# Attention and two feed-forward blocks on one core: one Mish session for chunks 0 and 1, in-products of chunk 2 by quarters, first transfers from two queues, other places for the attention calls

## The chip, the cores and the metric

The kernel runs on one core of a Trainium2 chip. A core has four compute engines that this text needs: TensorE (PE, matrix products, with weight loads on PEld), VectorE (DVE), ScalarE (ACT) and GpSimd (POOL), and a queue engine, SyncE (SP), that issues transfers. Each runs its own instructions in order, and they wait for each other by semaphores. The metric is the device time of one execution in microseconds.

## The reference, cut to what is computed

```
scores = q @ k.T / 8                     # 4 batches, 8 heads, 576 x 576, head size 64
mask:  heads 0..3 local (the last 32 positions), heads 4..7 strided (same position mod 32, not later)
attn = softmax(masked scores) @ v        # -> x, 2304 tokens x 512
h = x @ w_in;  g = h * tanh(softplus(h)) # Mish, 2048 wide
x = g @ w_out                            # 512
out = (silu(x @ w_gate) * (x @ w_val)) @ w_out2    # 1536 wide
```

Weights and activations are 32-bit; products are made from a high and a low part of each operand, so one product of the algebra is three on TensorE (`mm3`: high by high, high by low, low by high).

## The kernel before

Attention goes in 24 steps of six or eight blocks of 64 queries (local steps have 96 keys in a block, strided steps 64). Batch b has steps 6b to 6b+5: three for heads 0 to 3 (local), three for heads 4 to 7 (strided), and in the last batch the strided ones come first. One call of `at_pair` is a software pipeline over steps: call k computes scores of step k (`at_qk`), maxima with the mask added (`at_max`, VectorE), exponentials (`at_exp`, ScalarE); normalises step k-1 (`at_add` on GpSimd, `at_norm`: a reciprocal on VectorE, two multiplications on GpSimd); transposes step k-2 (`at_tr`, `at_copy`); and multiplies step k-3 with v (`at_pv`), splitting the result into `xh` (`at_hi`, a cast on ScalarE) and `xl` (`at_lo`, a subtraction on VectorE). The list `PAIR` fixes the order of these in a call, and so the order on each engine. Scores have two banks (`sc`), so the scores of a call wait until the maxima of the call before are read.

The first feed-forward block works on five chunks of tokens (512 each, the last 256) and four quarters of the hidden width. n = 5q + c counts quarter and chunk. For n = 0, 1, 2 the work is woven into the attention calls: `g1_step(n, f, kc)` adds a quarter kc of the contraction to h of hidden tile f (three products), and after kc = 3 `act_a` takes h out of its bank, because Mish needs another table on ScalarE than exp. Three banks (`mm`) serve both h and the out-products y. h goes to a tile `u` (four buffers); `act_m` loads the Mish table, applies Mish to four tiles and loads exp again; `g_hi` and `g_lo` split the result; `g2_mm` multiplies it with the out-weight.

Calls 0 to 14 come in a loop in which the tables `WSTEPS` and `GROUPS` say how many weight operations (`w_step`: four per weight tile, on VectorE, and one square on ScalarE) and which g1 steps follow a call. `KEEP` and `NWARM` are counts of idle products (`spin`) that keep TensorE at work while it has nothing. `DOS` runs deferred steps from the list `todo` (Mish of chunk 0 among them) at places in calls 13 and 14. After that, `fill` runs ahead of each g1 step or after each g2 product, counts itself, starts a call where its count is in `PAIR_AT`, and runs one to three deferred steps. From n = 3 (chunk 3) on there is no attention left and products follow each other.

K and Q of a pair of heads lie in one of four buffers, which are those of the accumulators `acc0` to `acc3` (`load_qk`, L298); `acc0` holds its last K and Q in call 7. The first transfers are all issued by SyncE, the masks (`cst`) first (L818 to L829).

Names in rows: `sc` scores, `pt` and `sm` exponentials and sums, `tp` and `ts` transposes, `xp` the product with v, `w`, `wtmp` and `raw` a weight tile, its work buffer and its bits, `h`, `u`, `g`, `y` as above, `wp` the spins. L92 is `mm3`; L83 and L88 are the high and low split, of whichever tile.

Of the kernel before, what the change touches and what calls it, by code (L numbers as in the profile page):

```python
# [20 lines left out]
LK = LB + STR  # L21
# [17 lines left out]
NWARM = 10  # L39
KEEP = {0: 2, 1: 3, 2: 4, 3: 4}  # L40
QK_SLOT = (0, 1, 2, 3, 0, 1, 2, 3, 1, 2, 3, 1, 2, 3, 1, 2)
GROUPS = {
# [11 lines left out]
}  # L54
WSTEPS = (0, 0, 4, 4, 3, 3, 2, 0, 1, 1, 2, 2, 2, 2, 0)
WFILL = 6
DOS = {13: (0, 2), 14: (1, 0, 2, 2)}
PAIR_AT = (0, 5, 13, 16, 19, 22, 26, 30, 34, 38, 42, 47)
# [5 lines left out]
def local_strided_attention__mish_moe__swiglu_kernel(  # L64
# [241 lines left out]
    def load_v(s):  # L306
        b, first, g, part = steps[s]
        t = sb.tile([128, 2, 4, 128], F32, tag="v", name="v", bufs=2)
        n = len(part) // 2
        for x in range(2):  # L310
            v_t[s, x] = t[:128 if first else LK, x, :n]
            nc.sync.dma_start(v_t[s, x], (v_str if first else v_loc)[b, 2 * g + x, :, :n])
# [159 lines left out]
    def of(do, h):  # L472
# [6 lines left out]
        (at_add, -1),  # L479
        (at_pv, -3),  # L480
# [6 lines left out]
        (at_norm, -1),  # L487
# [7 lines left out]
    SPLIT = 8  # L495
# [20 lines left out]
    us, gt = {}, {}  # L516
# [19 lines left out]
    def act_a(n, f, keep):  # L536

        nt = CHUNKS[n % NCH][1]
        p = h_ps.pop((n, f))[:, :nt]
        us[n, f] = u = sb.tile([128, 512], F32, tag="u", name="u", bufs=4)[:, :nt]  # L540
        if keep:
            if n:
                nc.vector.tensor_copy(u, p)
            else:
                nc.scalar.copy(u, p)
        else:
            nc.scalar.activation(out=u, in_=p, func=AF.Mish)  # L547
# [257 lines left out]
    with tc.manual_schedule():  # L805
# [27 lines left out]
        def act_all(n):  # L833
            todo.append(lambda n=n: act_m(n))
            for f in range(QF):
                todo.append(lambda n=n, f=f: g_hi(n, f))
                todo.append(lambda n=n, f=f: g_lo(n, f))

        def g1_step(n, f, kc):
# [3 lines left out]
            if kc == 3:  # L843
                act_a(n, f, True)
                if n == 0 and f == QF - 1:
                    act_all(0)

        for k in range(len(WSTEPS)):
# [3 lines left out]
            dos = list(DOS.get(k, ()))  # L852
            for x in (None,) + GROUPS.get(k, ()):
                if x:
                    g1_step(*x)
                do(dos.pop(0) if dos else 0)
        fills = [0]

        def fill():
# [3 lines left out]
            if fills[0] < WFILL + 2:  # L863
                w_lo(nc.vector)
                w_hi()
                w_step(fills[0] < WFILL)
            fills[0] += 1
            do(3 if len(todo) > 10 else 2 if len(todo) > DO2 else 1)

        g1s = [(n, f, kc) for n, fs_ in ((1, (3,)), (2, range(QF))) for f in fs_ for kc in range(4)]  # L870
        g1s.insert(0, (1, 2, 3))
        wfill = [0]
        for n in range(1, 3):
# [3 lines left out]
            todo.append(lambda n=n: act_m(n))  # L877
# [188 lines left out]
```

## Time and profile before

| | |
|---|---|
| median of 3 runs | 900.97 us (900.77 to 901.16) |
| the profiled execution | 902.88 us |
| its span, first to last instruction | 901.1 us |
| TensorE busy | 879.2 us (98%) |
| VectorE, ScalarE, GpSimd busy | 585.3, 385.6, 137.2 us |
| mean granted clock of TensorE | 0.99 of full speed |

A row of the order of time gives the start and the duration in microseconds, the engine, the line, the operation, what it writes and reads, how many in a row, and in brackets how long the engine had been idle and what ended that. Busy time of a pipelined TensorE overlaps a little between groups, so starts are the safer numbers. Full speed is 2.4 GHz; the lower level is 1.2 GHz, and a mean between is a mix of both.

### The profile page before, as it was taken

How to read it: one execution, taken by the hardware profiler on the slowest of the kernel's cores; microseconds unless marked ns; L12 is line 12 of the kernel's file. 1: busy time of each engine (PE TensorE's matmuls, PEld its weight loads, DVE VectorE, ACT ScalarE, POOL GpSimd, SP SyncE). 2: the span in 40 equal slices, each digit the busy share in tenths (PEclk: the TensorE clock that was granted, in tenths of full speed). 3: DMA queues.
4: the chain of work that ended last, by engine and by line, in shares of the span. 5: the costliest groups of instructions: out<-in, count | busy, mean ns of one | idle time of the engine just before them, and what ended most of it. 6: DMA issues, size and time to landing. Idle time of an engine off the chain costs nothing.

```text
span 901.1 us, 14264 instructions
## 1 busy us (share of the span) xinstructions
PE 879.2 (98%) x5283; PEld 731.8 (81%) x5283; DVE 585.3 (65%) x1272; ACT 385.6 (43%) x944; POOL 137.2 (15%) x156
## 2 busy tenths in 40 slices
PE   7898899999999999999999999999999999999998
PEld 4776677888888888888888888888888888888886
DVE  5787567669876887778384987856435635333534
ACT  6697865334443553343243643342323412322230
POOL 3232230000000000000021320311214312111211
PEclk9799999999999999999999999999999999999999
DMA  7765522435533554434009798665351553553222
GB/s 233 260 192 168 171 75 79 149 109 185 192 131 106 183 184 145 139 94 148 40 9 378 249 351 343 235 247 203 137 203 54 188 211 139 210 187 122 111 94 94
DMA packets 49509, 151.91 MB, mean 169 GB/s; under 512 B 5408, under 2 KB 13088, under 8 KB 49440
## 3 DMA queue, kind: packets, MB, share of 16 engines
q1 hardware_dynamic: 49440, 151.00, 48.0%
q8 instruction: 42, 0.69, 0.3%
q14 instruction: 27, 0.22, 0.1%
HBM read 114.80 MB, written 36.18 MB: 168 GB/s over the span
## 4 chain that ended last, share of the span: by engine, by line
PE 92%; ACT 4%; DVE 2%; issue 0%; POOL 0%; ACTq 0%; DVEq 0%; POOLq 0%
PE y L92 21%; PE h L92 21%; PE o L92 16%; PE cXg L92 7%; PE cXv L92 7%; PE c L92 4%; PE cZv L92 4%; PE cZg L92 4%; ACT pt L361 2%; PE xp L421 2%; PE cYv L92 2%; PE cYg L92 2%; PE sc L322 1%; PE tp L392 1%; PE wp L813 0%; DVE pt L347 0%
## 5 line engine op out<-in xcount | busy, mean ns | idle before, releaser
L92 PE MATMUL y<-g,w 128*128 128x512 f32 (+1 forms) x960 | 204.4, 370 | 3.0 <-ACT w L83 2.4
L92 PE MATMUL h<-xh,w 128*128 128x512 f32 (+1 forms) x640 | 190.8, 375 | 5.5 <-ACT xh L83 3.8
L92 PEld LDWEIGHTS y<-g,w 128*128 128x128 f32 x960 | 167.2, 189 | 33.8 <-ACT w L83 2.6
L92 PE MATMUL o<-wr,fs 128*128 128x512 f32 x648 | 149.6, 389 | 0.0
L92 PEld LDWEIGHTS o<-wr,fs 128*128 128x128 f32 x648 | 121.3, 188 | 25.0
L92 PEld LDWEIGHTS h<-xh,w 128*128 128x128 f32 x640 | 117.8, 191 | 27.5 <-ACT xh L83 4.4
L92 PE MATMUL h<-xl,w 128*128 128x512 f32 (+1 forms) x320 | 119.8, 375 | 2.6 <-DVE xl L88 2.6
L547 ACT ACTIVATE u<-h 128x512 f32<-128x512 f32 (+1 forms) x68 | 37.3, 548 | 140.3 <-PE h L92 140.3
L800 DVE TENSOR_TENSOR acc<-acc,o 128x512 f32<-128x512 f32 x90 | 61.4, 686 | 48.6 <-PE o L92 48.5
L88 POOL TENSOR_TENSOR fs<-k,fs 128x512 fp32r<-128x512 f32 x36 | 48.7, 1353 | 267.0 <-ACT fs L83 208.4
L92 PEld LDWEIGHTS h<-xl,w 128*128 128x128 f32 x320 | 61.1, 191 | 14.0 <-DVE xl L88 4.5
L361 ACT ACTIVATE pt<-pt,sm 128x64 f32<-128x64 f32 (+1 forms) x160 | 55.7, 350 | 17.2 <-DVE sm L347 17.1
L88 DVE TENSOR_TENSOR g<-u,g 128x512 fp32r<-128x512 f32 (+1 forms) x80 | 51.2, 661 | 16.7 <-ACT g L83 16.7
L83 ACT CAST fs<-k 128x512 fp32r<-128x512 f32 x36 | 22.4, 622 | 88.2 <-DVE k L755 37.6
L741 DVE TENSOR_TENSOR k<-cZg,k 128x512 f32<-128x512 f32 x12 | 8.3, 692 | 73.9 <-PE cZg L92 73.9
L92 PE MATMUL cXg<-T,wr 128*128 128x512 f32 x216 | 54.8, 389 | 0.0
L92 PE MATMUL cXv<-T,wr 128*128 128x512 f32 x216 | 54.8, 389 | 0.0
L88 POOL TENSOR_TENSOR B<-acc,B 128x512 fp32r<-128x512 f32 x6 | 8.3, 1391 | 300.3 <-ACT B L83 300.3
L83 ACT CAST ws<-wt 128x512 fp32r<-128x512 f32 x60 | 37.0, 616 | 35.6 <-DVE wt L225 31.7
L83 ACT CAST g<-u 128x512 fp32r<-128x512 f32 (+1 forms) x80 | 44.5, 574 | 15.6 <-PE y L92 15.4
L92 PEld LDWEIGHTS cXv<-T,wr 128*128 128x128 f32 x216 | 40.5, 188 | 8.4
L92 PEld LDWEIGHTS cXg<-T,wr 128*128 128x128 f32 x216 | 40.5, 188 | 8.5 <-DVE k L741 0.2
(103 smaller groups left out, 1326.1 us busy)
## 6 DMA issues: line engine op xcount, KB each, us to landing
raw<-in_w_dram SPq DMA_DIRECT2D x54, 512.0 KB, 3.7
wr<-wd_g_S SPq DMA_DIRECT2D x24, 512.0 KB, 7.2
wr<-wd_v_S SPq DMA_DIRECT2D x24, 512.0 KB, 7.5
wr<-wd_p SPq DMA_DIRECT2D x24, 512.0 KB, 4.5
wr<-wd_g_W SPq DMA_DIRECT2D x18, 512.0 KB, 6.4
wr<-wd_v_W SPq DMA_DIRECT2D x18, 512.0 KB, 7.2
qk<-in_qk_dram SPq DMA_DIRECT2D x14, 600.0 KB, 6.2
rawl<-in_w_dram SPq DMA_DIRECT2D x14, 512.0 KB, 5.6
```

What stands on the lines that cost most here:

```text
L83: nc.scalar.copy(hi, src)
L88: eng.tensor_tensor(out=lo, in0=src, in1=hi.bitcast(F32), op=ALU.subtract)
L92: nc.tensor.matmul(o, lhsT=lhs, rhs=rhs, start=first and i == 0, stop=last and i == 2, skip_group_check=more)
L322: nc.tensor.matmul(sc[h][x % 2 * 64:x % 2 * 64 + 64, x // 2 * w:(x // 2 + 1) * w], lhsT=t[64 * h:64 * h + 64, q0:q0 + 64], rhs=t[64 * h:64 ...
L361: nc.scalar.activation(out=pt[:, x], in_=pt[:, x], func=AF.Exp, scale=-1.0, bias=sm[:, 0, x:x + 1], accum_out=sm[:, 1, x:x + 1],)
L392: nc.tensor.transpose(tp[:, 128 * x:128 * x + 128], a, ident)
L421: nc.tensor.matmul(xp[64 * h:64 * h + 64, o:o + nq - skip], lhsT=vt[:, y % n, 64 * h:64 * h + 64], rhs=ts[:, c0 + skip:c0 + nq], start=Tru ...
L547: nc.scalar.activation(out=u, in_=p, func=AF.Mish)
L741: nc.vector.tensor_tensor(out=t, in0=p, in1=t, op=ALU.add)
L800: nc.vector.tensor_tensor(out=acc[c][:, t], in0=acc[c][:, t], in1=o, op=ALU.add)
```

## The change

Nothing of what is computed changes; order and places do.

- **Start.** Seven spins instead of ten. K of the first pair goes out first on SyncE; Q of the first pair, the first masks and a part of Q of the second go out on ScalarE's queue, ahead of its first table load.
- **Calls 0 to 14.** Call 4 has four spins, no g1 step, and a weight operation more; call 5 has all four of the first g1 steps. In calls 11 to 14 the steps of chunk 1 stand elsewhere, and (1,2,3) comes in call 14. In `PAIR` the reciprocal and the normalisation stand right after `at_add`, ahead of the scores.
- **Mish.** h of chunk 0 goes into one tile in the place of `acc0`, so `u` is free for chunk 1. Mish of chunk 0 is issued after call 14's products, three tiles of chunk 1 follow in the same session at fill 0, the fourth at fill 4; then exp is loaded. In between, the exponentials of step 15 are held back. Chunk 2's Mish no longer loads exp after it.
- **Fills.** Call 15 stays at fill 0; call 16 moves from fill 5 to 13 and the later ones lie between 16 and 49. g1 of chunk 2 goes by kc over f = 0, 1, 2, then f = 3.
- **v** of a step is loaded by one transfer in place of two.

```diff
-NWARM = 10
-KEEP = {0: 2, 1: 3, 2: 4, 3: 4}
+NWARM = 7
+KEEP = {0: 2, 1: 3, 2: 4, 3: 4, 4: 4}
 GROUPS = {
-    4: ((0, 0, 0),),
-    5: ((0, 1, 0), (0, 0, 1), (0, 1, 1)),
+    5: ((0, 0, 0), (0, 1, 0), (0, 0, 1), (0, 1, 1)),
...
-    13: ((1, 2, 1), (1, 0, 2), (1, 1, 2)),
-    14: ((1, 2, 2), (1, 0, 3), (1, 1, 3)),
+    13: ((1, 0, 2), (1, 1, 2), (1, 2, 2)),
+    14: ((1, 0, 3), (1, 1, 3), (1, 2, 3)),
 }
-WSTEPS = (0, 0, 4, 4, 3, 3, 2, 0, 1, 1, 2, 2, 2, 2, 0)
-WFILL = 6
-DOS = {13: (0, 2), 14: (1, 0, 2, 2)}
-PAIR_AT = (0, 5, 13, 16, 19, 22, 26, 30, 34, 38, 42, 47)
+WSTEPS = (0, 0, 4, 4, 4, 2, 2, 0, 1, 1, 2, 2, 2, 2, 2)
+WFILL = 4
+PAIR_AT = (0, 13, 16, 19, 22, 25, 28, 31, 35, 40, 45, 49)
...
+    held = [False]
+
     def at_exp(s, h):
+        if held[0]:
+            held.append((s, h))
+            return
...
         (at_add, -1),
+        (at_norm, -1),
         (at_pv, -3),
...
         (of(at_exp, 0), 0),
-        (at_norm, -1),
         (at_lo, -3),
...
-        us[n, f] = u = sb.tile([128, 512], F32, tag="u", name="u", bufs=4)[:, :nt]
+        if n:
+            u = sb.tile([128, 512], F32, tag="u", name="u", bufs=4)[:, :nt]
+        else:
+            if f == 0:
+                u0[0] = sb.tile([128, 4, 512], F32, tag="acc0", name="u")
+            u = u0[0][:, f]
+        us[n, f] = u
...
-    def act_m(n):
-        for f in range(QF):
+    def act_m(n, fs_=range(QF)):
+        for f in fs_:
             nc.scalar.activation(out=us[n, f], in_=us[n, f], func=AF.Mish)
+
+    def act_m_end():
         nc.scalar.preload_act_table_set(EXP)
+        held[0] = False
+        while len(held) > 1:
+            at_exp(*held.pop(1))
...
-        nc.sync.dma_start(cst[:, :192], consts[:, :192])
-        load_qk(0, ((QW, QW + 416), (0, 384), (384, QW), (QW + 416, QW + KW)))
-        load_qk(1, ((0, 192), (QW, QW + 224)))
+        load_qk(0, ((QW, QW + 416),))
+        nc.scalar.dma_start(qk_t[0][:, :384], qk[0, :, :384])
+        nc.scalar.dma_start(cst[:, :192], consts[:, :192])
+        load_qk(1, ())
+        nc.scalar.dma_start(qk_t[1][:, :192], qk[1, :, :192])
+        for i, c0, c1 in ((0, 384, QW), (0, QW + 416, QW + KW), (1, QW, QW + 224)):
+            nc.sync.dma_start(qk_t[i][:, c0:c1], qk[i, :, c0:c1])
...
+            for x in GROUPS.get(k, ()):
+                g1_step(*x)
+                if x == (1, 0, 3):
+                    act_m(0)
+                    held[0] = True
+        MISH = (
+            (lambda: g_hi(0, 0), lambda: g_hi(0, 1), lambda: act_m(1, (0, 1, 2))),
+            (lambda: g_hi(0, 2), lambda: g_lo(0, 0)),
+            (lambda: g_hi(0, 3), lambda: g_lo(0, 1)),
+            (lambda: g_lo(0, 2),),
+            (lambda: act_m(1, (3,)), act_m_end, lambda: g_lo(0, 3)),
+        )
...
-        g1s = [(n, f, kc) for n, fs_ in ((1, (3,)), (2, range(QF))) for f in fs_ for kc in range(4)]
-        g1s.insert(0, (1, 2, 3))
+        g1s = [(1, 3, kc) for kc in range(4)]
+        g1s += [(2, f, kc) for kc in range(4) for f in range(3)] + [(2, 3, kc) for kc in range(4)]
```

On ScalarE, at the end of call 13 before and of call 14 after, from the last exponentials on (`L551` and `L562` are Mish, `L552` and `L565` the load of exp). Before:

```order
L215 ACTIVATE w<-raw 128x512
L551 ACT_TABLE_LOAD
L551 ACTIVATE u<-u 128x512 x4
L552 ACT_TABLE_LOAD
L83 CAST g<-u 128x512
L83 CAST xh_70<-xp 128x14x17
L83 CAST xh_72<-xp 128x4x17
L361 ACTIVATE pt,sm<-pt,sm 128x96 x3
```

After:

```order
L562 ACT_TABLE_LOAD
L562 ACTIVATE u<-u 128x512 x4
L81 CAST xh_72<-xp 128x384
L81 CAST w<-wtmp 128x512
L405 COPY ts<-tp 96x256
L213 ACTIVATE w<-raw 128x512
L81 CAST g<-u 128x512 x2
L562 ACTIVATE u<-u 128x512 x3
L81 CAST g<-u 128x512 x2
L562 ACTIVATE u<-u 128x512
L565 ACT_TABLE_LOAD
L366 ACTIVATE pt,sm<-pt,sm 128x64 x8
```

The cast of `xh_70`, which h of chunk 1 reads, stood behind the session and now stands ahead of it; Mish of chunk 1 and the exponentials of step 15 now follow in one queue.

On VectorE, after the maxima of call 15. Before:

```order
L222 SCALAR_TENSOR_TENSOR wtmp<-raw,wtmp 128x512
L543 COPY u<-h 128x512
L225 SCALAR_TENSOR_TENSOR wtmp<-w,wtmp 128x512
L88 TENSOR_TENSOR g<-u,g 128x512
L216 TENSOR_SCALAR wtmp<-raw 128x512
```

After:

```order
L86 TENSOR_TENSOR w<-wtmp,w 128x512
L214 TENSOR_SCALAR wtmp<-raw 128x512
L217 SCALAR_TENSOR_TENSOR wtmp<-raw,wtmp 128x512
L86 TENSOR_TENSOR g<-u,g 128x512
L220 SCALAR_TENSOR_TENSOR wtmp<-raw,wtmp 128x512
L86 TENSOR_TENSOR g<-u,g 128x512
L223 SCALAR_TENSOR_TENSOR wtmp<-w,wtmp 128x512
L86 TENSOR_TENSOR g<-u,g 128x512
L554 COPY u<-h 128x512
```

Three of chunk 0's four `g` low parts were made ahead of these rows; now none is, and the copy of h(1,3) out of its bank stands last of nine.

On TensorE, from the last products of h(1,3) on. Before:

```order
L92 MATMUL h<-xh_70,w 128x512
L92 MATMUL y<-g,w 128x512 x3
L392 MATMUL tp<-cst,pt 96x128 x4
L421 MATMUL xp<-ts,v 64x64 x12
L322 MATMUL sc<-qk 64x64 x16
L392 MATMUL tp<-cst,pt 96x128 x2
L92 MATMUL y<-g,w 128x512 x24
```

After:

```order
L90 MATMUL h<-xh_70,w 128x512
L90 MATMUL y<-g,w 128x512 x30
L397 MATMUL tp<-cst,pt 96x128 x4
L426 MATMUL xp<-ts,v 64x64 x12
L322 MATMUL sc<-qk 64x64 x16
L397 MATMUL tp<-cst,pt 96x128 x2
L90 MATMUL y<-g,w 128x512 x9
```

Call 16 stood behind the first three out-products and now stands behind thirty.

## Rows read from the trace of the kernel before

**Rows 1.** Page, part 1: busy us, share of the span, instructions, by engine.

```profile
PE 879.2 (98%) x5283; PEld 731.8 (81%) x5283; DVE 585.3 (65%) x1272; ACT 385.6 (43%) x944; POOL 137.2 (15%) x156
```

**Rows 2.** Waits of TensorE, 0 to 200 us: total us, times, longest us.

```profile
PE tp L392 <- POOL pt L380: 4.5, 4, 1.6
PE h L92 <- ACT xh L83: 3.8, 1, 3.8
PE h L92 <- DVE xl L88: 2.6, 2, 2.0
PE y L92 <- ACT w L83: 2.4, 1, 2.4
PE h L92 <- DVE w L88: 1.2, 1, 1.2
...
PE y L92 <- DVE u L543: 0.5, 1, 0.5
PE h L92 <- ACT w L83: 0.5, 1, 0.5
```

**Rows 3.** Windows: length, then busy us of PE, PEld, DVE, ACT, POOL, clock, DMA.

```profile
12.00:28.00 16.00, 11.91 (x190) 8.40 (x190) 15.18 (x68) 12.91 (x58) 6.17 (x9) 0.85 0.82 268
28.00:44.00 16.00, 14.22 (x192) 11.38 (x192) 11.81 (x57) 9.99 (x47) 4.34 (x9) 0.83 0.72 239
```

**Rows 4.** Order of time, TensorE: the first product of chunk 3.

```profile
146.73 0.39 PE L92 MATMUL h<-xh,w 128*128 128x512 f32 x1
```

**Rows 5.** Order of time, TensorE, the start.

```profile
1.08 4.45 PE L813 MATMUL wp<-wz 128*128 128x512 bf16 x10 [1.08 <-POOL wz L806]
...
5.46 1.08 PE L322 MATMUL sc<-qk 64*64 64x96 f32 x24
```

**Rows 6.** Transfers, 0 to 20 us: KB each, us from issue to landing.

```profile
qk<-in_qk_dram SPq DMA_DIRECT2D x1, 208.0 KB, 2.8
```

**Rows 7.** Order of time, TensorE, calls 6 to 8: products with v, scores.

```profile
31.64 1.14 PE L421 MATMUL xp<-ts,v 128*64 128x54 f32 x32
...
36.70 1.77 PE L421 MATMUL xp<-ts,v 128*64 128x54 f32 x32
38.40 1.24 PE L322 MATMUL sc<-qk 64*64 64x96 f32 x24
...
43.47 0.72 PE L322 MATMUL sc<-qk 64*64 64x96 f32 x24
```

**Rows 8.** Order of time, TensorE: scores of calls 13 and 14.

```profile
64.78 0.73 PE L322 MATMUL sc<-qk 64*64 64x96 f32 x24
...
69.11 0.72 PE L322 MATMUL sc<-qk 64*64 64x96 f32 x24
```

**Rows 9.** Order of time, ScalarE, from call 13's last exponential on.

```profile
67.88 0.36 ACT L361 ACTIVATE pt<-pt,sm 128x96 f32<-128x96 f32 x1
...
68.93 1.28 ACT L551 ACT_TABLE_LOAD   x1
70.22 2.19 ACT L551 ACTIVATE u<-u 128x512 f32<-128x512 f32 x4
```

**Rows 10.** Order of time, TensorE, after its long waits, and undisturbed rows.

```profile
74.66 0.80 PE L92 MATMUL h<-xh,w 128*128 128x512 f32 x1 [3.77 <-ACT xh L83]
...
92.70 0.60 PE L392 MATMUL tp<-cst,pt 128*128 128x128 f32 x4
...
97.08 3.58 PE L92 MATMUL y<-g,w 128*128 128x512 f32 x9 [2.42 <-ACT w L83]
...
103.30 2.34 PE L92 MATMUL y<-g,w 128*128 128x512 f32 x9
...
110.32 1.01 PE L392 MATMUL tp<-cst,pt 128*128 128x128 f32 x4 [1.07 <-POOL pt L380]
```

**Rows 11.** Order of time, VectorE, 78 to 80 us: two full tiles.

```profile
78.47 0.69 DVE L543 COPY u<-h 128x512 f32<-128x512 f32 x1
79.07 0.68 DVE L88 TENSOR_TENSOR g<-u,g 128x512 fp32r<-128x512 f32 x1
```

More of the change, by code (lines that the diff above doesn't have):

```diff
@@ L307, in load_v @@
         b, first, g, part = steps[s]
-        t = sb.tile([128, 2, 4, 128], F32, tag="v", name="v", bufs=2)
         n = len(part) // 2
+        k = 128 if first else LK
+        t = sb.tile([128, 2, 4, 128], F32, tag="v", name="v", bufs=2)[:k, :, :n]
+        src = (v_str if first else v_loc)[b, 2 * g:2 * g + 2, :, :n]
+        nc.sync.dma_start(t, src.rearrange("x p n d -> p x n d"))
         for x in range(2):
-            v_t[s, x] = t[:128 if first else LK, x, :n]
-            nc.sync.dma_start(v_t[s, x], (v_str if first else v_loc)[b, 2 * g + x, :, :n])
+            v_t[s, x] = t[:, x]
     def at_qk(s):
@@ L494, in local_strided_attention__mish_moe__swiglu_kernel @@
     ]
-    SPLIT = 8
+    SPLIT = 9
     apos = [0]
@@ L514, in at_pair @@
                         do(a + lag)
-    us, gt = {}, {}
+    us, u0, gt = {}, [None], {}
     h_ps = {}
@@ L560, in g_hi @@
     def g_hi(n, f):
-        gt[n, f] = g = sb.tile([128, 2, 512], F32R, tag="g", name="g", bufs=6)
-        split_hi(nc.scalar, g[:, 0, :CHUNKS[n % NCH][1]], us[n, f])
+        gt[n, f] = sb.tile([128, 2, 512], F32R, tag="g", name="g", bufs=6)
+        split_hi(nc.scalar, gt[n, f][:, 0, :CHUNKS[n % NCH][1]], us[n, f])
     def g_lo(n, f):
@@ L832, in local_strided_attention__mish_moe__swiglu_kernel @@
         NA = NQ * NCH
[L833 to L837, printed above, removed]
         def g1_step(n, f, kc):
@@ L844, in g1_step @@
                 act_a(n, f, True)
-                if n == 0 and f == QF - 1:
-                    act_all(0)
         for k in range(len(WSTEPS)):
@@ L851, in local_strided_attention__mish_moe__swiglu_kernel @@
             w_step(WSTEPS[k])
[L852 to L856, printed above, removed]
+            for x in GROUPS.get(k, ()):
[10 more added lines that the diff above has]
+        )
         fills = [0]
@@ L866, in fill @@
                 w_step(fills[0] < WFILL)
+            for x in MISH[fills[0]] if fills[0] < len(MISH) else ():
+                x()
             fills[0] += 1
             do(3 if len(todo) > 10 else 2 if len(todo) > DO2 else 1)
-        g1s = [(n, f, kc) for n, fs_ in ((1, (3,)), (2, range(QF))) for f in fs_ for kc in range(4)]
-        g1s.insert(0, (1, 2, 3))
+        g1s = [(1, 3, kc) for kc in range(4)]
+        g1s += [(2, f, kc) for kc in range(4) for f in range(3)] + [(2, 3, kc) for kc in range(4)]
         wfill = [0]
@@ L876, in local_strided_attention__mish_moe__swiglu_kernel @@
                 g1_step(*g1s.pop(0))
-            todo.append(lambda n=n: act_m(n))
+            if n == 2:
+                todo.append(lambda: act_m(2))
             def fill2():
```

4 rows, old and new, of the table GROUPS are left out of this document.

## The prediction

> **What bounds the kernel now.** I read the page's first part, then the view of waits for TensorE, then windows of ten to sixteen microseconds, and only then the order of time. TensorE is busy for 879.2 of 901.1 us [rows 1]: the kernel is bound by its products, and all that a change of order can win is the time in which TensorE has none, plus the time in which it runs at the lower clock because it had none. Both lie ahead of 147 us, since the view of waits names nothing for TensorE later. The reader should see three kinds there [rows 2]. The two long ones, 3.8 us on `xh` and 2.4 us on a weight's high part, end on ScalarE. In both cases ScalarE had gone to Mish and back: a table load, four Mish, a table load, and the casts that TensorE wanted stood behind it. Then come waits on VectorE (`xl`, `w`, `u`: 2.6, 1.2, 0.5), and 4.5 us in four waits on GpSimd's normalisation. The first 44 us are bound otherwise: VectorE is busy for 15.18 of the 16 us from 12 to 28 [rows 3], and the mean granted clock is 0.85 and 0.83, so TensorE there pays for its own gaps.
>
> I write "call k" for the k-th call of `at_pair`: scores of step k, transposes of step k-2, the product with v of step k-3. "h(n,f,kc)" is one `g1_step`, three products; "y(n)" are the out-products of chunk n. The sum goes by where TensorE stands when it begins chunk 3, at 146.73 now [rows 4]; from there on the work is the same and no wait is left.
>
> **Part 1: start and calls 0 to 8.** Ten spins fill TensorE from 1.08 to 5.53, and the first scores start as they end, at 5.46 [rows 5]. Seven spins end at 1.08 + 7 x 0.43 = 4.1. The first K piece takes 2.8 us from issue to landing [rows 6] and is now issued first on its queue, with Q from ScalarE's queue beside it; no row shows a DMA from ScalarE, so I bound what is won there by nothing and by 1.3 us. I take 0.2, the low end, for this reason: `at_norm` is now ahead of `at_qk`, so VectorE's reciprocal of step k-1 stands ahead of the maxima of step k. In steady state it is ready by then. In calls 1 and 2 it isn't: it needs the whole of that step's exponentials, and VectorE, the engine that bounds the next 16 us, waits for them with the maxima queued behind. The four spins added to call 4 stand where TensorE waits for VectorE anyway: nothing.
>
> From call 2 to 5 VectorE runs back to back [rows 3]. The change takes nothing off it; one weight operation moves from call 5 to 4, and the low part of the third in-weight from call 6 to 5. That last move pays: TensorE's wait in call 6 for that weight (0.5 for its high part, 1.2 for its low part [rows 2]) goes, and with it the lower clock after it: the product with v takes 1.77 against 1.14, the scores 1.24 against 0.72 [rows 7]. Sum 1.7 + 0.6 + 0.5 = 2.8; with the start **3.0 won**, bounds 0 (VectorE is late all the same) and 4.1.
>
> **Part 2: calls 11 to 14.** One more group, (1,2,3), is fitted in ahead of the Mish; that is only moved. But h(1,0,2) and h(1,0,3) now stand first in calls 13 and 14, where (1,2,1) and (1,2,2) stood. Each needs the `xl` that VectorE writes in the same call, after the maxima. Three products have gone as its cover, 9 in 2.34 us [rows 10], so 0.78. Bounds 0 and 0.78 each; I take 0.55, **1.1 lost**.
>
> **Part 3: waits that go.** From call 14 to 146.73 TensorE's waits were 3.8 + 2.4 + 0.5 and 0.6 of the 2.6 on `xl` [rows 2], and 1.07 on GpSimd [rows 10]: 8.4. The 3.8 goes because Mish comes after call 14's exponentials; the 2.4 because the second session has no call behind it until fill 13; the 0.6 because chunk 2 is now taken quarter by quarter, three f for each kc, so that no kc is wanted in the call that makes it; the 1.07, which fell where only six products stood between two calls, because the reciprocal now starts a call's VectorE work (calls 18 and 19 again have six between them). The 0.5, on a copy of `u`, is part of what part 4 counts anew. **8.4 won**. The clock comes back with it: 9 products took 3.58 after the 2.4, against 2.34 [rows 10], so 1.24, about the same after the 3.8, and four transposes 1.01 against 0.60: **2.9 won**.
>
> **Part 4: the wait that comes.** TensorE's first y now follows closely on a longer queue. Counted from the start of call 14's scores: ScalarE's last exponential ends after 3.5 (67.88 + 0.36 - 64.78 [rows 8, 9]), say 3.7 with the copy that this step has; a table load 1.29 and four Mish 2.19 [rows 9] make 7.2, the cast of `xh` 7.65. VectorE then has, in this order, `xl` and four maxima (1.0), and eight full tiles at 0.60, by the starts at 78.47 and 79.07 [rows 11], and a half one: the weight's low part, three weight steps and a half, three `g` low parts, and the copy of h(1,3) out of its bank: 13.8. This copy frees the third `mm` bank, which y(0) needs for e = 2. TensorE meanwhile: 4.33 to the next scores [rows 8], 0.55 from part 2, 0.8 for scores and transposes, twelve products 2.9 (by 9 in 2.34 [rows 10], less the overlap of their ends): 8.6, and six products of y(0), 1.5. So it waits 13.8 - 8.6 - 1.5 = **3.7 lost**, in two pieces, plus the clock after it, **1.2** as above. Bounds: 2 if VectorE's tiles find the queue shorter, 5.5 if GpSimd and VectorE slow each other. Queued behind the waits: call 16's maxima stand behind the reciprocal of step 15, whose exponentials are held back over both sessions; they end some five microseconds after that copy (one Mish, a load, eight exponentials), about when TensorE gets to call 16 (24 products later), so I count nothing, up to 1 if late. The fourth bank of y(0) now waits for a copy behind call 16's VectorE work: **0.8 lost**.
>
> **Part 5, without a price.** One DMA per v pair in place of two: SP issues fewer, and TensorE never waited for v. Four table loads fewer (two to exp, two to Mish): 5.1 us of ScalarE, off the path except for those in part 3.
>
> ScalarE's load to first Mish is 1.29 us, with nothing between [rows 9]. The Trainium skill, "ScalarE: Activation LUTs", What ACT_TABLE_LOAD costs, gives a switch of set 1.28 us plus a drain of 1.38. The trace shows the load and no drain; by that page of the skill the y wait would be about 1.4 longer, 894.9, and that is a rival at 1 in 100.
>
> **Sum.** 3.0 - 1.1 + 8.4 + 2.9 - 3.7 - 1.2 - 0.8 = 7.5 us. The profiled execution took 902.88 us (span 901.1), which gives 895.4; it lay 1.9 above the median of 900.97, so the median to expect is 900.97 - 7.5 = **893.5**.
>
> **Rivals.**
>
> (b) VectorE is still the bound in the first 44 us and part 1 wins nothing: 896.5. For it: 15.18 of 16 us busy; against: after 28 us it is busy for only 11.81 of 16 [rows 3].
>
> (c) The stalls only regroup: ScalarE's and VectorE's queues are one behind the other, and the new wait is as long as the two old ones with their clock (8.7 in place of 4.9): 897.3.
>
> (d) Slower: from call 17 to 22 there are now 9, 9, 6, 9, 9, 9 products ahead of a call, and 12 ahead of 23; before, calls 21 to 23 had twelve. If the normalisation is late in each of these seven, as at 110.32, that costs 1.07 and 0.41 of clock a time [rows 10], 7 x 1.48 = 10.4: 903.9. It decides from six of the seven. For it: in calls 16 and 17 VectorE has some seven full tiles' worth of work, with the y copies and `g` low parts: 4.2 us at 0.60 [rows 11], of the 4.33 that a call with nine products takes. Against: call 13 had nine products and no such wait [rows 8].
>
> (e) The better way: the y wait 2 and the start 1.3: 890.7.
>
> **How the numbers follow.** Forecast 0.49 (own range 891 to 896), (b) 0.16, (c) 0.12, (d) 0.10, (e) 0.12, the skill's drain 0.01. Unknown costs at their good ends give 888.8, at their bad ends 899.8 without (d); I take 888.5 to 900. A measurement can tell about 0.2%, 1.8 us: faster 0.84, within it 0.07 (the worst of b and c together, or half of d), slower 0.09.
>
> **What would show it.** Right: the first scores before 4.7 us; no wait for a weight in call 6; one Mish session of four, then three and one, with two loads; TensorE's longest wait on y, ended by VectorE, first on a `g` low part and then on a copy of `u`, together 2 to 5.5 us; granted clock about 0.8 in the window after it; chunk 3 begun near 139. Wrong: waits on GpSimd in several of calls 17 to 23 (d), a second scores start no earlier and the eighth still near 43 (b), or a wait on y above 7 us (c).

## The result, and the profile after

| | before | after |
|---|---|---|
| median (runs) | 900.99 us (900.77 to 901.16; 4) | 892.59 us (891.13 to 893.61; 4) |
| the profiled execution | 902.88 us | 892.32 us |
| its span | 901.1 us | 890.2 us |
| TensorE's first product of chunk 3 | 146.73 us | 136.16 us |

The ratio is 0.9906 (95% interval 0.9889 to 0.9923): 8.4 us faster by the medians, where 7.5 was forecast. Between the two profiled executions it is 10.6, and all of it lies ahead of chunk 3: 146.73 - 136.16 = 10.57. The two figures differ because the profile of before was 1.9 us over its median and that of after 0.3 under its own. The four runs of after also spread more, 2.5 us against 0.4.

The page of after, part 1, beside [rows 1]:

```profile
PE 872.4 (98%) x5284; PEld 727.7 (82%) x5284; DVE 583.5 (66%) x1272; ACT 379.8 (43%) x940; POOL 136.0 (15%) x156
```

The waits of TensorE in the first 200 us of after (us in all, times, longest), beside [rows 2]:

```profile
PE tp L397 <- POOL pt L385: 4.1, 4, 1.6
PE h L90 <- DVE xl L86: 2.4, 3, 1.4
PE y L90 <- DVE u L554: 1.6, 1, 1.6
PE xp L426 <- DMA v<-in_v_str_dram: 1.5, 1, 1.5
...
PE y L90 <- DVE g L86: 1.1, 1, 1.1
PE y L90 <- DVE acc L609: 0.7, 1, 0.7
PE y L90 <- ACT g L81: 0.6, 1, 0.6
PE sc L322 <- DMA qk<-in_qk_dram: 0.5, 1, 0.5
```

The two long waits on ScalarE (`xh` 3.8, `w` 2.4) and those for a weight in call 6 (0.5 and 1.2) are gone. New are three waits on y with 3.2 us together, a fourth on `acc`, and two on transfers. The four on GpSimd have about their old sum, but all lie ahead of 23 us.

Windows of after (length, busy us of PE, PEld, DVE, ACT, POOL, granted clock, DMA share, GB/s); the first two answer to [rows 3]:

```profile
12.00:28.00 16.00, 11.60 (x192) 8.17 (x193) 15.36 (x69) 13.58 (x62) 5.77 (x11) 1.00 0.87 264
28.00:44.00 16.00, 14.51 (x235) 11.52 (x238) 12.14 (x63) 11.93 (x57) 5.30 (x11) 1.00 0.82 259
80.00:90.00 10.00, 10.00 (x91) 8.07 (x90) 2.73 (x17) 5.65 (x26) 1.43 (x3) 0.86 0.26 82
```

VectorE is as full in the first window as before, yet the clock is 1.00 where it was 0.85 and 0.83. The clock's loss now stands behind the waits on y.

TensorE of after in order of time, at the places that answer to [rows 4, 5, 7, 8, 10]:

```profile
4.22 0.72 PE L322 MATMUL sc<-qk 64*64 64x96 f32 x24
...
30.63 0.73 PE L322 MATMUL sc<-qk 64*64 64x96 f32 x24
...
34.07 1.14 PE L426 MATMUL xp<-ts,v 128*64 128x54 f32 x32 [1.50 <-DMA v<-in_v_str_dram]
...
39.41 0.72 PE L322 MATMUL sc<-qk 64*64 64x96 f32 x24
...
62.12 0.50 PE L90 MATMUL h<-xl,w 128*128 128x512 f32 x1 [0.49 <-DVE xl L86]
...
74.91 0.50 PE L90 MATMUL y<-g,w 128*128 128x512 f32 x1 [0.55 <-ACT g L81]
76.48 1.43 PE L90 MATMUL y<-g,w 128*128 128x512 f32 x5 [1.07 <-DVE g L86]
79.49 7.26 PE L90 MATMUL y<-g,w 128*128 128x512 f32 x24 [1.58 <-DVE u L554]
...
91.14 0.96 PE L90 MATMUL y<-g,w 128*128 128x512 f32 x3 [0.73 <-DVE acc L609]
...
136.16 0.39 PE L90 MATMUL h<-xh,w 128*128 128x512 f32 x1
```

Call 8's scores come 4.06 us earlier (43.47 - 39.41), and the stretch from there to chunk 3 is 6.51 shorter (103.26 and 96.75). The forecast had 3.0 and 4.5. Of the 4.06, 2.08 stand at call 6's scores (32.71 and 30.63), where the forecast had the start's 0.2. These scores in before:

```profile
32.71 0.73 PE L322 MATMUL sc<-qk 64*64 64x96 f32 x24
```

### The profile page after: what moved, and what is told of

It is laid out like the page before. It is cut to its first block, busy times and chain, and to the rows that moved or that the text cites. A ratio compares the mean times of both kernels' runs of the same rounds, so it can differ in the third digit from the quotient of the medians.

```text
span 890.2 us, 14236 instructions
## 1 busy us (share of the span) xinstructions
PE 872.4 (98%) x5284; PEld 727.7 (82%) x5284; DVE 583.5 (66%) x1272; ACT 379.8 (43%) x940; POOL 136.0 (15%) x156
## 4 chain that ended last, share of the span: by engine, by line
PE 94%; DVE 2%; ACT 2%; DMA 1%; issue 0%; POOL 0%; SPq 0%; ACTq 0%; DVEq 0%; POOLq 0%
PE y L90 22%; PE h L90 21%; PE o L90 17%; PE cXg L90 7%; PE cXv L90 7%; PE c L90 4%; PE cZg L90 4%; PE cZv L90 4%; PE xp L426 2%; PE cYv L90 2%; PE cYg L90 2%; ACT pt L366 1%; PE sc L322 1%; PE tp L397 1%; DMA v<-in_v_str_dram 1%; DVE pt L347 0%
## 5 line engine op out<-in xcount | busy, mean ns | idle before, releaser
L90 PE MATMUL h<-xh,w 128*128 128x512 f32 (+1 forms) x640 | 188.3, 371 | 0.0
```

What stands on the lines that cost most here:

```text
L90: nc.tensor.matmul(o, lhsT=lhs, rhs=rhs, start=first and i == 0, stop=last and i == 2, skip_group_check=more)
```

## The experiments

All start from the kernel after, and all but the last two change one thing or one place. Ratios are to the kernel before on the same chip; intervals are about 0.0015 to each side, 1.3 us, so small effects are read from the trace, between two fixed instructions, of one execution each.

**The start.** `b1_old_start` puts the old start back:

```diff
-NWARM = 7
+NWARM = 10
-        load_qk(0, ((QW, QW + 416),))
-        nc.scalar.dma_start(qk_t[0][:, :384], qk[0, :, :384])
-        nc.scalar.dma_start(cst[:, :192], consts[:, :192])
...
+        nc.sync.dma_start(cst[:, :192], consts[:, :192])
+        load_qk(0, ((QW, QW + 416), (0, 384), (384, QW), (QW + 416, QW + KW)))
+        load_qk(1, ((0, 192), (QW, QW + 224)))
```

> The changed kernel with the old start: ten spins, the masks first, all transfers from SyncE. My prediction gave the start 0.2 us, bounds 0 and 1.3; the changed kernel's trace has the first scores 1.24 us and the maxima of calls 1 and 2 0.6 and 1.0 us earlier than before. Theory A (the start carries through): first scores at 5.46, call 2's maxima at about 12.0, call 8's scores 0.6 to 1.3 us after 39.41, the time 0.6 to 1.3 us over 892.6. Theory B (VectorE or the transfers between 12 and 34 us set the pace, whatever the start): call 8's scores within 0.3 us of 39.41, the time unchanged.

Measured: 893.14 us, ratio 0.9914 (0.9900 to 0.9929). The first scores start at 5.46, 1.24 after those of the kernel after, call 6's at 32.14, 1.51 after, and call 8's at 40.41, 1.0 after. By the trace theory A holds; the medians, 0.6 apart, can't tell. VectorE between 12 and 30 us does not take the start's gain back; 0.5 of it is lost on the transfer of v, for which call 7 waits 1.50 in the kernel after and 0.99 here. Chunk 3 begins 1.35 later (137.51), but 0.4 of that lies behind call 15's scores, in a stretch that differs between executions without any edit there (below, calls 12 to 14).

**The place of the reciprocal.** `a4_norm_old`:

```diff
         (at_add, -1),
-        (at_norm, -1),
         (at_pv, -3),
...
         (of(at_exp, 0), 0),
+        (at_norm, -1),
         (at_lo, -3),
...
-    SPLIT = 9
+    SPLIT = 8
```

> The changed kernel with the reciprocal and the normalisation at their old place in a call, behind the first half of the maxima. Theory A (the prediction's): VectorE's maxima of calls 1 and 2 no longer wait behind the reciprocal, so that those of call 1 start at about 6.9 in place of 8.04 and the first calls win about 1 us; but with six to nine products between calls 17 and 23 TensorE waits for GpSimd there, about 1 us and 0.4 of clock in two to seven of them: 892.6 - 1 + 3 to 10, so 894 to 902. Theory B (the place of the reciprocal matters only at the start): no wait on GpSimd after 100 us, and the time falls to about 891.6. Theory C (the start is bound elsewhere): call 8's scores within 0.3 us of 39.41.

Measured: 894.91 us, ratio 0.9925 (0.9914 to 0.9937), 2.3 us slower than after by the medians, 1.7 by the ratios, whose intervals overlap. No theory holds whole. At the old place the maxima of call 1 do start earlier, at 7.55, and it wins nothing. VectorE and GpSimd of `a4_norm_old`, call 1:

```profile
7.55 0.26 DVE L347 CUSTOM_DVE_ANT_0 pt<-sc,cst 128x96 f32<-128x96 f32 x1 [0.90 <-PE sc L322]
...
8.41 0.19 DVE L382 RECIPROCAL sm<-sm 128x6 f32<-128x6 f32 x1 [0.24 <-POOL sm L377]
...
8.69 1.29 POOL L385 TENSOR_TENSOR pt<-pt,sm 128x384 f32<-128x384 f32 x2 [0.31 <-DVE sm L382]
```

`b2_groups` has the new place and a start of the same phase (first scores at 4.18 and 4.20). There:

```profile
8.39 0.19 DVE L382 RECIPROCAL sm<-sm 128x6 f32<-128x6 f32 x1 [1.76 <-POOL sm L377]
8.50 0.22 DVE L347 CUSTOM_DVE_ANT_0 pt<-sc,cst 128x96 f32<-128x96 f32 x1
...
8.67 1.29 POOL L385 TENSOR_TENSOR pt<-pt,sm 128x384 f32<-128x384 f32 x2 [0.31 <-DVE sm L382]
```

The reciprocal and the normalisation come at the same time in both, because both wait for GpSimd's sum of step 0's exponentials (at 8.14 and 8.12); the first transposes, which wait for the normalisation, start at 9.56 and 9.55. That chain sets the pace there, not the maxima. Later the new place pays: call 5's transposes start at 22.56 in place of 23.03, and with the old place TensorE's waits on GpSimd before 200 us are 6.6 us against 4.8, one of 0.69 in call 7 and one of 0.41 at 102.71 among them. Call 13's transposes, at 60.97, take 0.69 us in place of the 0.49 of after.

**The transfers of v.** `a3_two_v` loads a v pair by two transfers again:

```diff
...
-        nc.sync.dma_start(t, src.rearrange("x p n d -> p x n d"))
         for x in range(2):
-            v_t[s, x] = t[:, x]
+            v_t[s, x] = t[:128 if first else LK, x, :n]
+            nc.sync.dma_start(v_t[s, x], (v_str if first else v_loc)[b, 2 * g + x, :, :n])
```

> The changed kernel with each v pair loaded by two transfers again. Theory A (the load of a weight's bits and a K and Q pair, 1.1 MB, stand ahead of v on SyncE): the wait of 1.5 us in call 7 stays, at 1.2 to 2, and the time stays within 0.5 us of 892.6. Theory B (one transfer of 512 KB lands later than two of 256): the wait falls under 0.5, call 8's scores come 1 us or more before 39.41, and the time falls to about 891.5.

`b3_v_first` keeps one transfer but issues the fifth weight's bits behind it:

```diff
+    later = []
...
             wpend.append((key, w, tf))
-            w_load()
+            if apos[0] == 5:
+                later.append(w_load)
+            else:
+                w_load()
...
             load_v(s + 2)
+        while later:
+            later.pop()()
```

> The changed kernel in which one transfer is issued later: the bits of the fifth weight, which call 4's last weight operation issues ahead of call 5's K, Q and v, are issued behind that v. Theory A (the order on SyncE makes the wait of 1.50 for the v of step 4): the v is issued at about the same 26 us but has 512 KB less ahead of it, lands 1 us or more earlier than 34.0, and TensorE's wait for it is under 0.3. Call 8's scores come by 38.5 where the clock is as in the changed kernel, the time falls by about 1 to 891.6. Theory B (one transfer of 512 KB takes 7 to 8 us by itself): it still lands at 33.5 or later and the wait stays above 1.

`a2_weights33` undoes the move of a weight operation from call 5 to 4, and with it the same order on SyncE:

```diff
-WSTEPS = (0, 0, 4, 4, 4, 2, 2, 0, 1, 1, 2, 2, 2, 2, 2)
+WSTEPS = (0, 0, 4, 4, 3, 3, 2, 0, 1, 1, 2, 2, 2, 2, 2)
```

> The changed kernel with the weight operations of calls 4 and 5 as before (3 and 3 in place of 4 and 2). In the changed kernel TensorE waits 1.50 us in call 7 for the v of step 4, which no call did before; on SyncE the load of the next weight's bits now stands ahead of that v and of a K and Q pair, since the operation that frees its buffer moved to call 4. Theory A (order on SyncE): the v is issued earlier than 26.38 and lands before its product; the wait of 1.5 in call 7 goes. In its place a wait for the third in-weight of up to 1.7 us comes back in call 6, so the time is within 1.5 us of 892.6. Theory B (one large transfer of v takes longer than two small ones): the wait for v stays above 1 us. Theory C (VectorE's load is what counts): call 6's scores come later than 30.63 by 0.6 or more.

SyncE's queue in the kernel after, in order of time, its waits on VectorE from 18 to 32 us (in all, times, longest), and the operation of VectorE that ended the one ahead of these rows:

```profile
25.47 0.34 SPq L145 DMA_DIRECT2D raw<-in_w_dram  x1
25.85 0.43 SPq L301 DMA_DIRECT2D qk<-in_qk_dram  x1
26.38 4.74 SPq L310 DMA_DIRECT2D v<-in_v_str_dram  x2
...
SPq L145 <- DVE wtmp L220: 9.4, 3, 3.7
...
24.71 0.69 DVE L220 SCALAR_TENSOR_TENSOR wtmp<-raw,wtmp 128x512 int32<-128x512 int32 x1
```

and SyncE's queue in `b3_v_first`:

```profile
21.11 0.81 SPq L305 DMA_DIRECT2D qk<-in_qk_dram  x1
23.91 0.38 SPq L314 DMA_DIRECT2D v<-in_v_str_dram  x1
25.37 0.33 SPq L145 DMA_DIRECT2D raw<-in_w_dram  x1
```

In the kernel after the load of weight bits waits some 3 us in the queue, until VectorE has read the buffer that it overwrites (25.40), and K, Q and v stand behind it; v is issued at 26.38. With the weight bits behind it (`b3_v_first`) v is issued at 23.91, 2.5 us earlier. The transfers of that v, from issue to landing, in after, in `b3_v_first` and in `b2_groups` (below), which leaves SyncE's order and the size of v as in after:

```profile
v<-in_v_str_dram SPq DMA_DIRECT2D x1, 512.0 KB, 7.6
...
v<-in_v_str_dram SPq DMA_DIRECT2D x1, 512.0 KB, 7.4
...
v<-in_v_str_dram SPq DMA_DIRECT2D x1, 512.0 KB, 5.9
```

The transfer takes hardly less time with 512 KB fewer ahead of it (7.4 and 7.6); it is issued earlier, lands at about 31.3 in place of 34.0, and the wait is gone: from call 6's scores to call 7's it takes 3.16 us (30.51 to 33.67) in place of 4.51 (30.63 to 35.14), chunk 3 begins at 135.35, and the time is 891.57, ratio 0.9900 (0.9883 to 0.9918). That is theory A's result, on record as 891.6; but the issue of v, which it expected at about 26 us, comes at 23.91: what is won is the earlier issue, and a shorter transfer is not seen.

The wait has no fixed price. `b2_groups` issues the v at 26.82, undivided and behind the weight bits; it lands 5.9 us later, at 32.7, and call 7's product starts at 33.13 with no wait in the view. `b4_y_direct` and `c2_spins8`, with the same order, wait 1.09 and 1.12.

So `a3_two_v` doesn't settle theory B. Its wait falls to 0.28 (the view names VectorE for it) and its product starts at 33.29, although its first half is issued 0.4 later than v in after. But that half lands after 6.3 us, at 33.1, later than the whole v of `b2_groups`, and up to that product the two kernels differ only in v. What the size of the piece does is not shown. Its time is 892.72, ratio 0.9908 (0.9894 to 0.9923). The Trainium skill, "Perfetto Trace Analysis", DMA Optimizations, says that splitting a transfer into smaller chunks may let some of them start sooner; no run here shows that apart from these differences between executions.

`a2_weights33`: 892.97 us, ratio 0.9913 (0.9898 to 0.9928), so the time alone tells nothing. Its profile is of its slowest run (896.4), and shows the other side: v issued at 25.40 and no wait for it, but 0.54 and 1.17 us for a weight in call 6, as before, a clock of 0.59 from 36 to 40, and call 8's scores at 43.03. The weight move wins those waits and pays with a v that comes later.

**The spins of call 4.** `a1_no_spins` takes them out, `c2_spins8` has eight:

```diff
-KEEP = {0: 2, 1: 3, 2: 4, 3: 4, 4: 4}
+KEEP = {0: 2, 1: 3, 2: 4, 3: 4}
```

> The changed kernel without the four spins of call 4. My prediction priced them at nothing; but in the changed kernel's trace the granted clock from 12 to 44 us is 1.00 where it was 0.85 and 0.83. Theory A: the spins hold the clock. Then without them the clock falls to about 0.5 to 0.75 somewhere between 22 and 32 us, the products of h(0,0,0) to h(0,1,1) take about twice as long, and call 8's scores come 1 to 2 us later than 39.41; the time is 1 to 2 us over 892.6. Theory B: the clock is held by the earlier start and by the weight that no longer comes late in call 6, and the spins do nothing: clock 0.97 or more, call 8's scores within 0.3 us of 39.41, the time unchanged.

```diff
-KEEP = {0: 2, 1: 3, 2: 4, 3: 4, 4: 4}
+KEEP = {0: 2, 1: 3, 2: 4, 3: 4, 4: 8}
```

> The changed kernel with eight spins in call 4 in place of four. In call 5 TensorE waits 1.5 to 1.8 us for GpSimd behind those spins; in the five profiles with four spins and the changed weight operations that ran freely, the clock after that wait stayed at 1.00 in some and fell to about 0.5 in others, and without spins it fell. Theory A (idle products are what holds it): eight spins, 2.1 us, fill that wait without delaying the transposes (call 5's at 22.1 to 22.6), the clock is 1.00 from 20 to 44 us, the mean clock of all runs is 0.995 or more and the time 892 to 892.6. Theory B (something earlier decides, such as the start's phase): the clock still falls in 24 to 28 us in a run whose first scores took 1.24. Theory C: the spins delay the transposes by 0.3 us or more and the time rises to 893.

Windows of `a1_no_spins`:

```profile
24.00:28.00 4.00, 4.00 (x53) 3.38 (x51) 3.83 (x14) 3.02 (x13) 1.34 (x2) 0.50 0.94 315
28.00:32.00 4.00, 4.00 (x39) 3.19 (x38) 2.94 (x13) 2.21 (x11) 1.30 (x3) 0.75 0.95 360
```

and of `c2_spins8`:

```profile
24.00:28.00 4.00, 2.75 (x47) 1.96 (x41) 3.83 (x14) 3.02 (x13) 1.30 (x2) 1.00 0.92 326
28.00:32.00 4.00, 3.80 (x66) 3.17 (x67) 3.18 (x14) 2.82 (x14) 2.12 (x5) 1.00 0.92 349
```

Without spins TensorE is at 1.2 GHz from 24 to 28 us, and call 6's scores come at 32.32, 1.7 us later than in the kernel after. Of these, 0.4 lie ahead of the stretch: call 5's transposes start at 22.53 in place of 22.12. In `b2_groups`, `a3_two_v` (four spins) and `c2_spins8` (eight) they start at 22.56 and 22.57, and call 6's scores at 31.05, 31.07 and 31.08. So from an equal start call 6 comes 1.25 us later without the spins, as theory A has it. That is one profile, and four spins are no guarantee: in `a2_weights33`, with a weight operation more in call 5, the clock is 0.50 there too, and call 6's scores come at 32.32.

Full clock is not needed for that. With eight spins the clock is 1.00 from 24 to 28 us; with four it varies between executions, where the code up to call 6 differs in the start or in v at most: 1.00 in the profiles of after, `b1_old_start`, `b3_v_first` and `c1_all`, 0.87 in `b4_y_direct` (0.50 from 20 to 24), 0.57 in `a3_two_v` and `b2_groups`. Yet `b2_groups` at 0.57 reaches call 6 as early as `c2_spins8` at 1.00, which spends what it gained in a wait of 1.45 for the `xl` of h(0,0,1); in both, the product that reads it starts at 28.2. There VectorE sets the pace; without spins that product starts at 29.19.

In the medians the spins hardly show: 893.36, ratio 0.9909 (0.9897 to 0.9922), and 892.45, ratio 0.9904 (0.9889 to 0.9920). One reason can be seen: without spins the late v no longer delays anything, and call 8's scores come only 0.7 later than in after. `c2_spins8` still has runs from 890.8 to 894.2, and a mean clock of 0.993 in one of them, against the 0.995 expected of all.

**Calls 12 to 14.** `b2_groups`:

```diff
-    12: ((1, 1, 1), (1, 2, 1)),
-    13: ((1, 0, 2), (1, 1, 2), (1, 2, 2)),
-    14: ((1, 0, 3), (1, 1, 3), (1, 2, 3)),
+    12: ((1, 1, 1),),
+    13: ((1, 2, 1), (1, 0, 2), (1, 1, 2)),
+    14: ((1, 2, 2), (1, 0, 3), (1, 1, 3), (1, 2, 3)),
```

> The changed kernel with the steps of calls 12 to 14 rotated as they stood before: (1,2,1) and (1,2,2) first in calls 13 and 14, so that h(1,0,2) and h(1,0,3) have three products as cover. Theory A (the prediction's 1.1 us in two waits): the waits of 0.49 and 0.46 on xl go. The first is won (call 14's scores 0.4 to 0.5 earlier counted from call 12's); the second lies between call 14's scores and the out-products, whose wait follows ScalarE's and VectorE's queues behind those scores, and comes back there: the sum of the waits on y grows by about 0.45. Time 892.1. Theory B (all of it is won): the sum of the waits on y stays at 3.2 (0.55 + 1.07 + 1.58), time 891.6.

Measured: 891.31 us, ratio 0.9894 (0.9879 to 0.9908). Both waits go: from call 12's scores to call 15's it takes 12.86 us in place of 13.73. From there to call 16's scores it takes 17.81 in place of 17.40, and the waits on y are 2.3 in all in place of 3.2, with the clock lower behind the first two. But that is not this edit's doing. `b1_old_start` and `b3_v_first`, in which calls 12 to 14 stand as in after, take 17.78 and 17.76 for the same stretch, with the same rows. The 24 out-products of `b1_old_start` and of `b2_groups`:

```profile
80.48 7.63 PE L90 MATMUL y<-g,w 128*128 128x512 f32 x24 [0.67 <-DVE u L554]
...
78.03 7.63 PE L90 MATMUL y<-g,w 128*128 128x512 f32 x24 [0.67 <-DVE u L554]
```

In both, and in `b3_v_first`, the five products ahead of them take 2.34 to 2.36 us in place of 1.43, and the wait for `u` is that much shorter. So 0.87 is won up to call 15, and whether some of it comes back behind (theory A) or none (theory B) can't be told from this run: from call 12 to chunk 3 it takes 0.47 less than in after (78.86 and 79.33) and 0.8 less than in `b1_old_start` and `b3_v_first`.

**The wait on y.** `b4_y_direct` takes Mish of h(1,3) straight out of its bank, ahead of the other three of chunk 1, and moves the weight operations of fills 0 to 3 one fill on:

```diff
-                act_a(n, f, True)
+                act_a(n, f, (n, f) != (1, 3))
...
-            (lambda: g_hi(0, 0), lambda: g_hi(0, 1), lambda: act_m(1, (0, 1, 2))),
-            (lambda: g_hi(0, 2), lambda: g_lo(0, 0)),
-            (lambda: g_hi(0, 3), lambda: g_lo(0, 1)),
-            (lambda: g_lo(0, 2),),
-            (lambda: act_m(1, (3,)), act_m_end, lambda: g_lo(0, 3)),
+            (lambda: g_hi(0, 0), lambda: g_hi(0, 1)),
+            (lambda: g_lo(0, 0),),
+            (lambda: g_lo(0, 1),),
+            (),
+            (lambda: g_hi(0, 2), lambda: g_hi(0, 3), lambda: g_lo(0, 2)),
+            (lambda: act_m(1, (0, 1, 2)), lambda: g_lo(0, 3)),
+            (act_m_end,),
...
-            if fills[0] < WFILL + 2:
+            if fills[0] < WFILL + 3:
...
-                w_step(fills[0] < WFILL)
+                w_step(0 < fills[0] < WFILL + 1)
```

> The changed kernel with another order around the first out-products: Mish of h(1,3) is taken straight out of its bank, ahead of the other three Mish of chunk 1, so VectorE's copy (0.68) and the wait for it go; and the weight operations of fills 0 to 3 stand one fill later, each behind a low part of g. Nothing of the work is left out. Theory A (the prediction's part 4: VectorE's queue and that copy set the y wait): the waits 1.07 and 1.58 fall to 0.5 and under 0.3, and 1 us or more of the 1.6 us of clock behind them (24 products in 7.26, at full clock about 5.6) comes back: 3 us earlier at chunk 3, time 889.5 to 890.5. Theory B (the wait moves on): the held exponentials or the last low part are late in their turn, a new wait of 2 us stands in call 16 or behind the 18th out-product, and the time stays within 0.8 of 892.6.

Measured: 888.79 us, ratio 0.9875 (0.9858 to 0.9892). VectorE of the kernel after, the last of its queue ahead of the third wait:

```profile
78.16 0.68 DVE L86 TENSOR_TENSOR g<-u,g 128x512 fp32r<-128x512 f32 x1
78.76 0.68 DVE L554 COPY u<-h 128x512 f32<-128x512 f32 x1
```

The copy ends at 79.44 and TensorE goes on at 79.49. TensorE of `b4_y_direct`:

```profile
75.44 6.91 PE L90 MATMUL y<-g,w 128*128 128x512 f32 x29 [0.89 <-DVE g L86]
...
87.22 0.96 PE L90 MATMUL y<-g,w 128*128 128x512 f32 x3 [1.22 <-DVE acc L609]
...
132.24 0.39 PE L90 MATMUL h<-xh,w 128*128 128x512 f32 x1
```

One wait of 0.89 is left of 3.2, and 29 products take 6.91 at full clock. From call 15's scores to call 16's it takes 13.32 us in place of 17.40; 0.48 is given back by chunk 3, which is what the wait for the fourth bank grew by (1.22 in place of 0.73). Theory A. The edit changes two things at once, the copy and the order of the queue, so it shows what both are worth together. And some 1.5 of the 4.08 is clock that `c2_spins8` had back without it: 15.91 us from call 15's scores to call 16's, with the three waits in place.

**Together.** `c1_all` joins `b4_y_direct`, `b2_groups`, `b3_v_first` and `a3_two_v`; `c3_all_spins8` has eight spins in call 4 as well.

> The changed kernel with four edits of this study together: Mish of h(1,3) straight out of its bank and the weight operations a fill later, the steps of calls 12 to 14 rotated, the fifth weight's bits issued behind v, and v by two transfers. Theory A (each edit takes away a wait of its own): chunk 3's first product came 3.9, 1.1 and 0.8 us earlier with the first three alone; with 0.5 to 0.9 of the second and 0.8 to 1.1 of the third still there when the first is in, chunk 3 begins at 130.5 to 131 and the time is 887 to 887.5. Theory B (they share a bound, VectorE's queue ahead of the out-products): no more than the first edit alone, chunk 3 at 132, the time 888.5 to 889.

> The kernel with the four edits together (c1), and eight spins in call 4. Theory A (spins hold the clock): clock 1.00 from 20 to 44 us, the time equal to c1's or up to 0.7 below it, with a smaller spread. Theory B: no difference in clock or spread from c1.

Measured: 887.59 us, ratio 0.9851 (0.9837 to 0.9865), with chunk 3 at 130.97; and 887.52, ratio 0.9846 (0.9833 to 0.9859). Theory A for `c1_all`: chunk 3 begins 5.19 us earlier than in after, and by stretches the gains stand side by side: 0.75 up to call 8's scores (v), 0.88 from call 12's to call 15's (the rotated steps), 3.57 from there (y), where `b4_y_direct` alone has 3.60. Both are faster than before and after. What the eight spins add is not shown: the median is the same, the profile of `c1_all` has a clock of 1.00 from 20 to 44 us with four, and the wider spread of its four runs (887.5 to 888.9, against 887.1 to 887.6) comes from one of them.

Not undone by themselves were the one Mish session, which is read from the traces of before and after alone, and the order of chunk 2 by quarters: with the calls where they now stand, the old order would read parts of `xh` that a later call writes.

## Why the prediction held, and where its steps did not

The time, 892.59, lies 0.9 from the forecast, and the better rival (e) at 890.7 farther. Chunk 3 begins at 136.16, earlier than the "near 139" that was to be seen. That the times agree to 0.9 is in part luck: the gain was worked out in one execution of before and taken off a median 1.9 us below it, and between the two profiled executions the gain is 10.6, not 7.5. By steps:

- **The start: 0.2 taken; 1.5 measured at call 6's scores, 1.0 at call 8's** (`b1_old_start`). The step that failed is "VectorE, the engine that bounds the next 16 us, waits for them with the maxima queued behind". It does wait (1.76 us), but maxima that come earlier win nothing there, because the transposes wait for the same exponentials by way of the normalisation (`a4_norm_old`). A queue behind a wait is a cost only if somebody waits for what is in it.
- **The weight move: the waits of 0.5 and 1.2 went**, as forecast (`a2_weights33` brings them back).
- **The four spins: "nothing" was too low.** In the one profile without them the clock stays down longer between 24 and 32 us (`a1_no_spins`), and from an equal start call 6's scores come 1.25 us later. Start and spins don't add up: together they win 2.08 there against before, with the other changes of that stretch.
- **"TensorE never waited for v" is where the price was missed.** It was true of the kernel before and no argument for after: calls that come earlier meet transfers that don't. The weight operation that moved to call 4 issues a load, which passed a K and Q pair and v on SyncE and waits there for VectorE; the prediction counted its VectorE time and not its transfer. Price: 1.50 us in the profile of after, nothing with the old order of issue (`b3_v_first`), and 0 to 1.12 in other executions with the new one.
- Part 1 as a whole: 3.0 forecast, 4.06 measured. By call 6's scores 2.08 was won where 0.2 was forecast, and from there to call 8's 1.98 (10.76 and 8.78), where 2.8 was: the waits of 1.8 went, the clock behind them gave 1.5 in place of 1.1, and 1.50 for v came; 0.2 is left over.
- **Calls 13 and 14: 1.1 lost, 0.95 measured** (0.49 and 0.46). Without the two waits call 15 comes 0.87 earlier (`b2_groups`), and in `c1_all` none of that is lost behind it.
- **The waits that go, 8.4, are gone; the clock that comes back with them was counted too low.** The sum of part 3 counts only the products right behind each long wait, 1.24 twice. The rows behind them in before (rows 10 have the products):

```profile
77.51 0.81 PE L392 MATMUL tp<-cst,pt 128*96 128x128 f32 x4
...
100.46 1.05 PE L392 MATMUL tp<-cst,pt 128*128 128x128 f32 x4
101.44 1.30 PE L421 MATMUL xp<-ts,v 128*64 128x54 f32 x32
```

By starts, the six products and four transposes behind the wait of 3.8 lost 1.55 (74.66 to 78.25, against 1.51 and 0.53 at full clock in after), and the nine products, four transposes and the product with v behind that of 2.4 lost 1.81 (97.08 to 102.67, against 2.18, 0.53 and 1.07): 3.4 in place of 2.5. The third clock term, 0.41 for the transposes at 110.32, was won but is no clock: the granted clock is 1.00 from 110.3 to 111.3, and the four start while GpSimd is still normalising. Two more sets in before, in calls 12 and 13, are stretched in the same way, at a clock of 1.00: 0.91 and 0.69 in place of 0.60 and 0.49 in after, some 0.5 by their starts, for which the forecast had nothing. The reciprocal's old place brings one of them back (`a4_norm_old`). With 8.4, 3.4, 0.4 and 0.5, less 0.95, 3.20, 0.73 and 1.5 for what came, the stretch from call 8 to chunk 3 should be 6.3 shorter; it is 6.51.
- **The new wait on y: 3.7 forecast, 3.20 measured** (0.55 + 1.07 + 1.58), on the two causes named, a low part of `g` and then the copy of `u`, and a short one ahead of them on ScalarE. `b4_y_direct` shows that the two together make the waits. The fourth bank: 0.8 and 0.73.
- **The clock behind it: 1.2 forecast, 1.5 in the profile.** It is no fixed price. `c2_spins8` has the same three waits (0.57, 1.06, 1.59), and its 24 products behind them ran at a clock of 1.00:

```profile
79.57 5.74 PE L90 MATMUL y<-g,w 128*128 128x512 f32 x24 [1.59 <-DVE u L554]
```

After took 7.26 for them, at a clock of 0.53 from 79.5 to 83. Of the nine profiles with these products and waits `c2_spins8` is the only one that kept the clock; from the first of the five products to call 16's transposes it takes 8.58 us, the others 10.1 to 10.8. Differences of this size, without an edit, may be what spreads the runs of after; that is not shown.
- **Held exponentials: nothing**, as forecast. **No drain** of ScalarE at the table load either; ScalarE of the kernel after at the session's end:

```profile
79.47 0.63 ACT L562 ACTIVATE u<-u 128x512 f32<-128x512 f32 x1 [0.58 <-DVE u L554]
80.12 1.28 ACT L565 ACT_TABLE_LOAD   x1
81.42 0.35 ACT L366 ACTIVATE pt<-pt,sm 128x64 f32<-128x64 f32 x1
```

The load starts as Mish ends and exp 1.30 after it. The 1.38 of drain that the Trainium skill, "ScalarE: Activation LUTs", What ACT_TABLE_LOAD costs, adds doesn't show in this trace either.
- **The rivals.** (b), the start wins nothing: refuted by 4.06. (c), the stalls regroup: the waits on y and their clock are 4.7, not 8.7. (d), late normalisation in calls 17 to 23: no wait on GpSimd there. Only with the reciprocal at its old place does one of 0.41 appear.

## What to carry to other kernels

When work is moved earlier, list for each of its operations the transfer that it issues, what that transfer passes in its queue, and what it waits for there; "never waited for" holds only as long as the consumer comes no earlier. Before charging a wait with the instructions queued behind it, look who waits for those: if their reader depends on the same event by another way, they cost nothing. And where a bank must be freed, let the engine that needs the data next read it from the bank in place of copying it out. And before a wait is read as what an edit did, look at the same stretch in runs that leave it alone.

## What the runs showed of the hardware

- Idle products in a stretch without work went with a higher clock behind them: mean granted clock from 24 to 28 us 0.50 without spins in call 4 (before, `a1_no_spins`), 0.50 to 1.00 with four (0.50 in `a2_weights33` and `a4_norm_old`, the rest as listed above), 1.00 with eight (`c2_spins8`, `c3_all_spins8`).
- About the same waits at the same place left the clock low in eight profiles and at 1.00 in one: from the first of five products to the end of 24 more 10.1 to 10.8 us, and 8.58 in `c2_spins8`.
- A load that waits in SyncE's queue holds back those behind it: v issued at 26.38 behind the weight bits, which waited for VectorE until 25.40, and at 23.91 ahead of them; the transfer itself took 7.6 and 7.4 us.
- One transfer of 512 KB, issued behind the same loads, took 7.6 us to land in after and 5.9 in `b2_groups`.
- GpSimd's two multiplications of 128x384 took 1.29 us ahead of VectorE's maxima (after, 15.91) and 2.23 behind their first half (`a4_norm_old`, 16.63).
